# Twelve of sixteen weight conversions moved from the attention stage into the first layer after it, and the w_out conversions spread over 28 slots

## Chip, cores and metric

One core of one Trainium2 chip runs the whole program. The metric is the device time of one launch in microseconds, lower is better. Engines are named as the profile names them: PE (TensorE; PEld is its weight load), DVE (VectorE), ACT (ScalarE), POOL (GpSimd), SP (the engine that issues the DMAs here).

## The reference

Three stages follow each other. All arithmetic is float32, and the weights arrive as float64.

```python
scores = scale * np.matmul(q, k.transpose(0, 1, 3, 2))       # 4 batches, 8 heads, 576 x 576, head size 64
decay = cum[:, :, :, None] - cum[:, :, None, :]              # cum: running sum of log f
scores = np.where(causal, -1000000000.0, scores + decay)
attn = softmax(scores); out = np.matmul(attn, v)

h = x @ w_in                                                 # 2304 tokens, 512 -> 2048
g = h * np.tanh(softplus(h))
x = (g @ w_out)                                              # 2048 -> 512

a = x @ w1; b = x @ w2                                       # 512 -> 1024
h = a * b @ w3                                               # 1024 -> 1024
return (h @ w_out2)                                          # 1024 -> 512
```

## The kernel before, in words

The kernel has two phases. `phase_a` does the attention in 16 pairs of heads, four *slots* to a pair (`NU = 4`), and four slots more at the end. `phase_b` does the rest in two passes over half the tokens each; in the first of these passes `first_layer` multiplies x by w_in for the last two batches.

**A slot of phase A** (`slots`, L679 on of the file as it was) issues one third of a pair's scores and softmax (`score`: PE L339, DVE L360 to L367, ACT L370), the transposes of the block before (`turn`: PE L407, then copies out of PSUM on ACT and DVE, both L422), in every fourth slot the product with v and its scaling (`pv`: PE L441; `x_rows`: DVE L452, which needs the reciprocal sums `R`, sent to DRAM and back, L387 to L394), and *filler*: matmuls of later layers that PE does beside the softmax (`plan`: 24 to a slot, from slot 37 on 12, from slot 53 on 12 in every third slot). From slot 37 on the filler is `l1_unit` (L524), x times w_in for the second batch.

**A weight conversion** turns one piece of 128 x 512 numbers from float64 into float32. The float64 words are loaded as pairs of int32 (`cv_load`, L121, 512 KB). ACT scales the upper word (`cv_exp`, L132), three DVE instructions put sign, exponent and mantissa bits together (`cv_bits`, L140 to L142), and then either the result is stored to a scratch tensor (`cv_store`, L149, 256 KB) or it is used at once. In the trace the raw words of w_out are `cvru` and the result is `cvu`; for w1 and w2 they are `cvrv` and `cvv`.

**Slots are given to conversions by a table** in `phase_a`. `job(s, ...)` puts the load into slot s-1, ACT's part into slot s+lag, and the last step into slot s+lag+1. The loop that matters gives the 16 pieces of w_out and then the 16 pieces of w1 and w2 one after the other:

```python
for i in range(32):
    s = W_OUT_SLOT + int(W_OUT_STEP * i)      # 30 + int(1.08 i): slots 30 to 46, then 47 to 63
```

After each second w_out piece `sums_of` (POOL, L803 to L806) and two `build` calls form the seven operands of a Strassen-like product (ACT L822, POOL L823, store `ws<-pt` or `ws<-bs`, L824, 256 KB each) for a later layer. The operands pass through five staging places, so that ACT's L822 waits for the store that used its place before.

**The first layer of phase B** runs seven products for each of eight units m (`m_layer`, `m_order`: for each m the products 5, 6, 2, 3, 7, then product 1 of the next m, then product 4). A product is 12 matmuls. Products 1, 6, 7 and 4 of a unit accumulate in one PSUM bank; between them ACT copies it (L990, L994) or DVE adds it (L1000) to `Cx`. So product 4 cannot begin before DVE's add of product 7, and the only work of PE in between is product 1 of the next unit. Products 2 and 3 are added by DVE at L996 and L998. Beside this DVE forms the next unit's operand sums (`s_sums`, `sr` tiles, L1045 to L1050), ACT and POOL split them (`s_build`, L1057 and L1058), and the operands of the layer behind (`k_begin`, `g_l`, `y`) are begun. The pieces of w1 and w2 are read back from the scratch tensor only in the layer after the next (`gate_load`).

Order on an engine: PE's order is the order of the code; for the other engines and for SP's DMA queue the framework chooses the order when the kernel is built, within the priorities that the code gives. Each engine then runs its list in that order, and SP issues the DMAs one behind the other.

Of the kernel before, what the change touches and what calls it, by code (L numbers as in the profile page):

```python
# [9 lines left out]
F32 = mybir.dt.float32  # L10
F32R = mybir.dt.float32r
BF16 = mybir.dt.bfloat16
I32 = mybir.dt.int32
AF = mybir.ActivationFunctionType
# [9 lines left out]
NPAIR = NH // 2  # L24
# [8 lines left out]
NU = 4  # L33
# [15 lines left out]
L1_BOTH = 6  # L49
W_IN_STEP = 0.8  # L50
W_OUT_SLOT = 30
W_OUT_STEP = 1.08
L1_S = (21, 37)
SHARE = (26, 24, 22, 24)

# [9 lines left out]
def f32(ap):  # L65
    return ap.bitcast(F32)
# [4 lines left out]
F64_EXP = 2.0 ** -112  # L71
# [3 lines left out]
class Kernel:  # L75
# [79 lines left out]
    def rows(self, w, m):  # L155

        return w[128 * m:128 * m + 128]

    def l1_bank(self):
        self.nl1 += 1  # L160
        return self.ps_l[self.nl1 % len(self.ps_l)]
# [414 lines left out]
    def phase_a(self):  # L576
# [41 lines left out]
        def at(s, fn, *a):  # L618
            misc.setdefault(s, []).append((fn, a))
# [3 lines left out]
        def job(s, key, src, fin, *a, lag=1):  # L623
            at(max(0, s - 1), self.cv_load, key, src)
            conv.setdefault(s + lag, []).append(key)
            at(s + lag + 1, fin, *a)
# [4 lines left out]
        jobs = [(f"i{m}", self.cols(self.w_in, m), self.win_split, m) for m in range(DFF // 128)]  # L631
        for i, j in enumerate(jobs):
            job(W_IN_SLOT + int(W_IN_STEP * i), *j)
        for i in range(32):
            f = i % 16
            s = W_OUT_SLOT + int(W_OUT_STEP * i)
            if i < 16:
                u = i // 2
                job(s, f"u{u + 8 * (i % 2)}", self.rows(self.w_out, u + 8 * (i % 2)), int, lag=2)
                if i % 2:  # L640
                    at(s + 3, self.sums_of, 0, u)
                    for k in range(2):
                        at(s + 4 + k, self.build, 0, u, k)
            else:
                key, src = f"v{f}", self.cols((self.w1, self.w2)[f % 2], f // 2)
                job(s, key, src, self.cv_store, key, self.w12_scr[f], lag=2)
        at(32, self.x_places, 1)
        for p in range(4, 8):
            for half, s in ((0, (32, 33, 34, 36)), (1, (38, 38, 39, 40))):
# [1 line left out]
        for p in range(NPAIR):  # L651
            s = NU * p
# [407 lines left out]
    def first_layer(self, cover):  # L1060

        nc = self.nc
        T, self.vs = {}, {}
        self.sp = [[self.w_ring(f"sp{i}_{j}")[:, :1024] for j in range(2)] for i in range(2)]
        self.tmp = self.t_tile("tmp", F32).rearrange("p (k r w) -> p k r w", k=2, r=2)
        self.s_sums(0)
        self.x_operands(T, (1, 5))
        self.s_build(0, 0)
        self.x_operands(T, (6, 2))
        self.s_build(0, 1)  # L1070
        self.x_operands(T, (3, 7, 4))
        cover()

        def get(m, o):
            if o in (1, 2, 4):
                return self.wi[m + 8 if o == 4 else m], 0 if o == 1 else 256, 512
            return self.sp[m % 2][o in (7, 3)], 512 if o in (6, 3) else 0, 256

        def post(m, o, d, ps):
            if o == 3:  # L1080
                t = self.y[m] = self.big(0, f"y0_{m}")
                nc.scalar.activation(t.rearrange("p (r h w) -> p h r w", r=2, h=2), d[:, 0:2], AF.Mish)
            elif o == 4:
# [152 lines left out]
```

## Time and profile before

| | |
|---|---|
| median of 3 runs | 1009.26 us (1008.63 to 1011.7) |
| the profiled execution | 1007.64 us, of which its span 1005.8 us |
| PE busy | 896.9 us (89%) |
| DVE busy | 655.7 us (65%) |
| ACT busy | 502.3 us (50%) |
| POOL busy | 434.7 us (43%) |
| DMA | 185.99 MB, mean 185 GB/s |
| chain that ended last | PE 56%, DVE 13%, DMA 10%, ACT 5%, issue 4%, POOL 3% |

The busy shares are means over a program of unlike stages. PE is busy all through phase B and through the middle of phase A, and idles at the start, in the last third of phase A and where phase B begins. So the profile is read by stretches: which engine waits in this stretch, and what ended its wait. The attention stage ends at about 404 us, the first layer of phase B at about 523 us.

### The profile page before, as it was taken

The numbers are of one execution on the slowest core, as the hardware profiler recorded it, in microseconds if no ns is written. First come the engines' busy times: TensorE is split into PE (matmuls) and PEld (weight loads), VectorE is DVE, ScalarE is ACT, GpSimd is POOL, SyncE is SP. The second block draws the span as 40 slices with busy tenths as digits, with TensorE's granted clock in tenths as the row PEclk, the third lists the DMA queues.
The fourth block names the chain that finished last, engine by engine and source line by source line (L and its number), as shares of the span: only waits on it lengthen the run. The fifth ranks groups of instructions, "written<-read, shape, count | busy, mean of one in ns | idle before, by whom it ended". The sixth has DMA issues, their size and how long they took to land.

```text
span 1005.8 us, 17588 instructions
## 1 busy us (share of the span) xinstructions
PE 896.9 (89%) x6336; PEld 817.9 (81%) x6336; DVE 655.7 (65%) x1126; ACT 502.3 (50%) x1089; POOL 434.7 (43%) x414
## 2 busy tenths in 40 slices
PE   0699999999788678779999897899999989999998
PEld 0367767888566557769999897899999989999998
DVE  5997786647675656995327739666468954744472
ACT  2566675756665544435534445544464354422143
POOL 4657775325876100633304558455055453410042
PEclk9899999999989789989999999899999999999999
DMA  8457678748898974100045454754977435455551
GB/s 244 144 167 232 206 228 271 201 148 256 285 310 282 301 223 159 60 7 1 1 156 180 131 185 160 280 201 169 340 285 231 162 130 168 148 167 168 166 172 71
DMA packets 129350, 185.99 MB, mean 185 GB/s; under 512 B 12064, under 2 KB 75696, under 8 KB 129264
## 3 DMA queue, kind: packets, MB, share of 16 engines
q1 hardware_dynamic: 129264, 184.88, 56.6%
q8 instruction: 50, 0.82, 0.3%
q14 instruction: 36, 0.29, 0.1%
HBM read 129.33 MB, written 55.42 MB: 184 GB/s over the span
## 4 chain that ended last, share of the span: by engine, by line
PE 56%; DVE 13%; DMA 10%; ACT 5%; issue 4%; POOL 3%; SPq 1%; DVEq 0%; ACTq 0%; POOLq 0%
PE ps_x L985 15%; PE ps_x L913 11%; PE ps_z L985 7%; PE ps_y L913 5%; PE ps_z L913 5%; PE ps_l L524 5%; PE ps_y L985 4%; DMA cvrv<-in_w_dram 2%; DMA ws<-pt 2%; PE ps_s L339 2%; DVE g_l L886 1%; DMA cvri<-in_w_in_dram 1%; DMA cvru<-in_w_out_dram 1%; POOL pt L823 1%; PE ps_t L407 1%
## 5 line engine op out<-in xcount | busy, mean ns | idle before, releaser
L886 POOL TENSOR_TENSOR g_l<-y,g_h 128x576 fp32r<-128x576 f32 x48 | 74.9, 1563 | 88.8 <-ACT g_h L884 62.3
L524 PE MATMUL ps_l<-x,wi 128*128 128x288 f32 x672 | 104.4, 312 | 2.8 <-ACT h L531 2.8
L524 PEld LDWEIGHTS ps_l<-x,wi 128*128 128x128 f32 x672 | 96.4, 199 | 11.2 <-issue 6.0
L913 PE MATMUL ps_x<-g_h,ws 128*128 128x288 f32 x512 | 92.8, 299 | 2.4 <-ACT g_h L884 2.1
L886 POOL TENSOR_TENSOR h_l<-ab,h_h 128x576 fp32r<-128x576 f32 x24 | 35.7, 1487 | 126.6 <-ACT h_h L884 114.4
L884 ACT CAST g_h<-y 128x576 fp32r<-128x576 f32 x96 | 63.9, 674 | 52.9 <-PE ps_x L913 28.4
L886 DVE TENSOR_TENSOR g_l<-y,g_h 128x576 fp32r<-128x576 f32 x48 | 53.1, 1110 | 50.0 <-ACT g_h L884 46.3
L913 PEld LDWEIGHTS ps_x<-g_h,ws 128*128 128x128 f32 x512 | 76.8, 191 | 3.7 <-ACT g_h L884 2.8
L370 ACT ACTIVATE P<-P,sum 128x256 f32<-128x256 f32 (+3 forms) x112 | 70.4, 631 | 16.7 <-DVE sum L367 10.4
L339 PE MATMUL ps_s<-raw 64*128 64x128 f32 (+3 forms) x256 | 53.0, 493 | 17.2 <-DVE xr L452 10.1
L913 PE MATMUL ps_x<-g_l,ws 128*128 128x288 f32 x256 | 56.5, 302 | 11.1 <-DVE g_l L886 8.3
L339 PE MATMUL ps_s<-aug 64*128 64x128 f32 (+3 forms) x128 | 38.2, 576 | 24.7 <-DVE cvo L141 22.0
L985 PE MATMUL ps_x<-T,gs 128*128 128x288 f32 x384 | 55.6, 301 | 4.5 <-ACT Cg L990 3.7
L985 PEld LDWEIGHTS ps_x<-T,gs 128*128 128x128 f32 x384 | 53.3, 193 | 5.0 <-ACT Cg L990 3.9
L985 PE MATMUL ps_x<-T,ws 128*128 128x288 f32 x384 | 54.3, 296 | 2.3 <-ACT x L941 1.4
L360 DVE CUSTOM_DVE_ANT_0 P<-ps_s,m 128x256 f32<-128x256 f32 (+2 forms) x96 | 49.3, 552 | 8.6 <-PE ps_s L339 8.1
L985 PEld LDWEIGHTS ps_x<-T,ws 128*128 128x128 f32 x384 | 52.0, 188 | 3.0 <-ACT x L941 1.7
L407 PE MATMUL ps_t<-ident,P 128*128 128x128 f32 x288 | 41.4, 281 | 14.6 <-ACT pt L422 14.6
L913 PEld LDWEIGHTS ps_x<-g_l,ws 128*128 128x128 f32 x256 | 41.6, 191 | 13.0 <-DVE g_l L886 9.7
L422 DVE COPY pt<-ps_t 128x128 f32<-128x128 f32 (+1 forms) x64 | 29.6, 483 | 32.1 <-PE ps_t L407 31.8
L884 ACT CAST h_h<-ab 128x576 fp32r<-128x576 f32 x48 | 32.0, 674 | 36.9 <-PE ps_x L913 17.8
L490 PE MATMUL ps_l<-wo,w3h 128*128 128x512 f32 x128 | 45.4, 424 | 4.9 <-POOL wo L111 2.9
(269 smaller groups left out, 2445.0 us busy)
## 6 DMA issues: line engine op xcount, KB each, us to landing
ws<-ws SPq DMA_DIRECT2D x112, 512.0 KB
ws<-pt SPq DMA_DIRECT2D x67, 256.0 KB
ws<-gs SPq DMA_DIRECT2D x56, 256.0 KB
h_scr<-h SPq DMA_DIRECT2D x64, 144.0 KB
y<-h_scr SPq DMA_DIRECT2D x16, 576.0 KB
cvrt<-in_w3t_dram SPq DMA_DIRECT2D x16, 512.0 KB
cvri<-in_w_in_dram SPq DMA_DIRECT2D x16, 512.0 KB
cvru<-in_w_out_dram SPq DMA_DIRECT2D x16, 512.0 KB
```

Source lines behind the costliest of these rows:

```text
L339: mm(ps[:, 512 * hh:512 * hh + n], t[r, q0:q0 + 128], t[r, 0:n], start=first, stop=not first)
L360: dve = ttr(P[hh][:, :n], ps[:, 512 * hh:512 * hh + n], self.m1[:, 512 - n:], -0.125, 3.0e38, ALU.add, ALU.min, st[hh])
L370: ins = nc.scalar.activation(t[:, :n], t[:, :n], AF.Exp, bias=b, scale=-1.0, accum_out=self.sums[:, i:i + 1])
L407: tr(self.ps_t[hh][:, o + 128 * k:o + 128 * k + 128], P[:, 128 * k:128 * k + 128], self.ident)
L422: return copy(dst[:, 0:c + 1, 128 * c:128 * c + 128], src)
L490: mm(o, w, x, start=i == 0, stop=i == 23)
L524: mm(o[:, :TB], w, x, start=i == 0, stop=i == 11)
L823: nc.gpsimd.tensor_tensor(lo, x, f32(hi), ALU.subtract)
L884: self.nc.scalar.copy(hi, raw)
L886: eng.tensor_tensor(lo, raw, f32(hi), ALU.subtract)
L913: mm(ps[:, r, :TB], w[:, 256 * a + 128 * e:256 * a + 128 * e + 128], ops[i][b][:, r], start=o in (1, 5, 2) and f == 0 and (a, b) == (0, 0) ...
L985: mm(bank[:, r, :TB], w[:, i:i + 128], T[o, k][:, b, r], start=o in (1, 2, 5) and (k, a, b) == (0, 0, 0), stop=(k, a, b) == (1, 1, 0), ski ...
```

## The change

The 16 pieces of w_out are now spread over slots 30 to 57 (`W_OUT_STEP` 1.8). Of the pieces of w1 and w2 only the first four (`V_SOON`) are converted in phase A, in slots 56, 58, 60 and 62. The other twelve are converted in `first_layer`, two in each unit from the second to the seventh. The raw words of an even piece go into `tmp`, a tile that the layer's operand preparation no longer needs by then (one tile, so that the next load waits until the piece before is converted); those of an odd piece go into two half tiles (`vw`) of a ring of 12, and the odd conversions are done in halves. The results (`vt`) come from the same ring, which also holds the `sr` tiles. All DMAs stay on SP's queue.

```diff
-W_OUT_STEP = 1.08
+W_OUT_STEP = 1.8
+V_SOON = 4
...
+    def v_load(self, f):
+
+        src = self.v_src(f)
+        if f % 2 == 0:
+            self.vw[f] = [self.tmpw[:, :1024]]
+            self.nc.sync.dma_start(self.tmpw[:, :1024].rearrange("p (c w) -> p c w", c=4), src)
+            return
+        self.vw[f] = [self.x_tile(f"vw{f}_{i}", I32)[:, :512] for i in range(2)]
+        for i, raw in enumerate(self.vw[f]):
+            self.nc.sync.dma_start(raw.rearrange("p (c w) -> p c w", c=2), src[:, 2 * i:2 * i + 2])
+
+    def v_convert(self, f):
+
+        out = self.x_tile(f"vt{f}", F32)[:, :512]
+        raws = self.vw.pop(f)
+        n = 512 // len(raws)
+        for i, raw in enumerate(raws):
+            t = out[:, n * i:n * i + n]
+            self.cv[f, i] = raw, t
+            hw = raw.rearrange("p (n w) -> p n w", w=2)[:, :, 1]
+            self.nc.scalar.activation(t, f32(hw), AF.Copy, scale=F64_EXP)
+            self.cv_bits((f, i))
+        self.nc.sync.dma_start(self.w12_scr[f], out)
...
-        for i in range(32):
-            f = i % 16
+        for i in range(16):
             s = W_OUT_SLOT + int(W_OUT_STEP * i)
...
-                key, src = f"v{f}", self.cols((self.w1, self.w2)[f % 2], f // 2)
-                job(s, key, src, self.cv_store, key, self.w12_scr[f], lag=2)
+        for f in range(V_SOON):
+            job(NU * NPAIR - 8 + 2 * f, f"v{f}", self.v_src(f), self.cv_store, f"v{f}", self.w12_scr[f])
...
+            f = V_SOON + 2 * m
+            if o == 1 and m and f <= 16:
+                self.v_convert(f - 2)
+            if o == 1 and f < 16:
+                self.v_load(f)
+                self.v_load(f + 1)
+            if o == 3 and m and f <= 16:
+                self.v_convert(f - 1)
```

PE's list is the same in both kernels, instruction for instruction. The other lists change in phase A from slot 30 on and in the first layer. Line numbers of the changed kernel are 26 to 29 higher.

**Place 1, SP's queue late in phase A.** `R12` and `R13` are the reciprocal sums that DVE's L452 waits for, `cvrv` a load of raw words of w1 or w2, `w12_scr` the store of a converted piece, `aug`, `raw` and `va` the inputs of a coming pair. Before, around pair 12:

```order
L149 DMA w12_scr_65<-cvv3_3482 128x512
L121 DMA cvrv7_3574<-in_w2_dram 128x4x256
L316 DMA aug0_93<-cum_scr_67 2x576
L314 DMA aug0_93<-cum_scr_67 2x576
L317 DMA aug0_93<-cum_scr_67 2x64
L306 DMA raw1_92<-in_qk_dram 64x512
L318 DMA aug1_94<-cum_scr_67 2x512
L532 DMA h_scr_61<-h1_0_1_3570 128x288
L303 DMA raw1_92<-in_qk_dram 64x2x576
L392 DMA R12_3576<-inv_scr_66 64x576
L393 DMA R12_3576<-inv_scr_66 64x512
L394 DMA R12_3576<-inv_scr_66 64x64
```

With the change, around pair 13, where the loads of the four early pieces stand:

```order
L416 DMA inv_scr_66<-inv13_3581 9x128
L421 DMA R13_3627<-inv_scr_66 64x576
L422 DMA R13_3627<-inv_scr_66 64x512
L423 DMA R13_3627<-inv_scr_66 64x64
L850 DMA ws0_62<-pt_86 256x1x256 x3
L122 DMA cvrv2_3715<-in_w1_dram 128x4x256
L850 DMA ws0_62<-bs0_6_3_3621 128x512
L150 DMA w12_scr_65<-cvv0_3588 128x512
L122 DMA cvrv3_3796<-in_w2_dram 128x4x256
L353 DMA va15_3802<-in_v_dram 128x4x128
```

Before, piece 7 was loaded here ahead of pair 12's sums; now only piece 2 is loaded after pair 13's, and stores of w_out operands (`ws0`) stand in a place where there were none.

**Place 2, DVE at the start of the first layer**, the adds of products 2, 3 and 7 of unit 0 (`Cx_0` with `ps_y`, `ps_z`, `ps_x0`). Before:

```order
L996 TENSOR_TENSOR Cx_0_4303<-Cx_0_4303,ps_y_4089 128x576
L1050 TENSOR_TENSOR sr1_3_4320<-sr1_0_4317,sr1_2_4319 128x256
L1048 TENSOR_TENSOR sr2_2_4414<-sr2_2_4414,sr2_0_4412 128x256
L886 TENSOR_TENSOR TX4_1_4178<-tmp_4097,TX4_1_4178 128x576
L998 TENSOR_TENSOR Cx_0_4303<-Cx_0_4303,ps_z_4090 128x576
L1047 TENSOR_TENSOR sr3_2_4524<-sr3_1_4523 128x256
L1049 TENSOR_TENSOR sr3_3_4525<-sr3_0_4522,sr3_1_4523 128x256
L1045 TENSOR_TENSOR sr4_0_4632<-wi4_1424 128x512
L1045 TENSOR_TENSOR sr4_1_4633<-wi12_1877 128x512
L1000 TENSOR_TENSOR Cx_0_4303<-Cx_0_4303,ps_x0_4087 128x576
```

With the change:

```order
L1071 TENSOR_TENSOR sr2_1_4322<-wi10_1808 128x512
L1074 TENSOR_TENSOR sr1_2_4223<-sr1_2_4223,sr1_0_4221 128x256
L1022 TENSOR_TENSOR Cx_0_4207<-Cx_0_4207,ps_y_3993 128x576
L1073 TENSOR_TENSOR sr2_2_4323<-sr2_1_4322 128x256
L1075 TENSOR_TENSOR sr2_3_4324<-sr2_0_4321,sr2_1_4322 128x256
L912 TENSOR_TENSOR TX4_1_4082<-tmp_4001,TX4_1_4082 128x576
L1076 TENSOR_TENSOR sr1_3_4224<-sr1_0_4221,sr1_2_4223 128x256
L1074 TENSOR_TENSOR sr2_2_4323<-sr2_2_4323,sr2_0_4321 128x256
L1024 TENSOR_TENSOR Cx_0_4207<-Cx_0_4207,ps_z_3994 128x576
L1026 TENSOR_TENSOR Cx_0_4207<-Cx_0_4207,ps_x0_3991 128x576
```

The operand sums of units 3 and 4 that stood ahead of the add of product 7 now come later, since the ring of their tiles is shared with the conversions.

**Place 3, DVE in the middle of the first layer**, around the adds of unit 3. Before:

```order
L996 TENSOR_TENSOR Cx_2_4508<-Cx_2_4508,ps_y_4089 128x576
L998 TENSOR_TENSOR Cx_2_4508<-Cx_2_4508,ps_z_4090 128x576
L1000 TENSOR_TENSOR Cx_2_4508<-Cx_2_4508,ps_x0_4087 128x576
L879 TENSOR_TENSOR y0_2_4601<-y0_2_4601 128x2x288
L880 TENSOR_TENSOR y0_2_4601<-y0_10_4654,y0_2_4601 128x2x288
L996 TENSOR_TENSOR Cx_3_4618<-Cx_3_4618,ps_y_4089 128x576
L998 TENSOR_TENSOR Cx_3_4618<-Cx_3_4618,ps_z_4090 128x576
L1000 TENSOR_TENSOR Cx_3_4618<-Cx_3_4618,ps_x1_4088 128x576
```

With the change (`vt10`, `vt11` are pieces 10 and 11, `tmp` and `vw11` their raw words):

```order
L1022 TENSOR_TENSOR Cx_3_4569<-Cx_3_4569,ps_y_3993 128x576
L1071 TENSOR_TENSOR sr6_0_4845<-wi6_1502 128x512
L1071 TENSOR_TENSOR sr6_1_4846<-wi14_2017 128x512
L141 TENSOR_SCALAR vt10_4724<-vt10_4724 128x512
L141 TENSOR_SCALAR vt11_4808<-vt11_4808 128x256 x2
L1024 TENSOR_TENSOR Cx_3_4569<-Cx_3_4569,ps_z_3994 128x576
L1073 TENSOR_TENSOR sr6_2_4847<-sr6_1_4846 128x256
L1075 TENSOR_TENSOR sr6_3_4848<-sr6_0_4845,sr6_1_4846 128x256
L142 SCALAR_TENSOR_TENSOR vt10_4724<-tmp_4001,vt10_4724 128x512
L142 SCALAR_TENSOR_TENSOR vt11_4808<-vw11_0_4600,vt11_4808 128x256
L142 SCALAR_TENSOR_TENSOR vt11_4808<-vw11_1_4601,vt11_4808 128x256
L1026 TENSOR_TENSOR Cx_3_4569<-Cx_3_4569,ps_x1_3992 128x576
```

Before, the three adds stood one behind the other; now operand sums and parts of two conversions stand between them.

## Rows read from the trace of the kernel before

**Rows 1.** Busy time by stretch (columns: PE, PEld, DVE, ACT, POOL, clock, DMA share, GB/s)

```profile
200.00:244.00 44.00, 44.00 (x346) 38.76 (x344) 23.81 (x64) 24.82 (x76) 17.61 (x23) 1.00 0.62 190
244.00:334.00 90.00, 74.86 (x523) 59.23 (x520) 60.04 (x155) 60.11 (x182) 59.29 (x76) 0.93 0.90 291
334.00:404.00 70.00, 54.20 (x369) 41.52 (x367) 42.97 (x113) 31.54 (x92) 1.46 (x2) 0.88 0.69 218
...
442.00:523.00 81.00, 80.08 (x584) 79.85 (x585) 39.49 (x62) 38.67 (x58) 19.85 (x14) 0.97 0.07 26
```

**Rows 2.** What PE waited for, 244 to 404 us (total us, times, longest)

```profile
PE ps_t L407 <- ACT pt L422: 14.6, 7, 4.2
PE ps_s L339 <- DVE xr L452: 10.1, 4, 4.7
PE ps_s L339 <- DMA cvrv<-in_w_dram: 2.0, 1, 2.0
```

**Rows 3.** PE's timeline (start, us, in brackets the idle time before and its releaser)

```profile
251.94 2.81 PE L441 MATMUL ps_s<-pt,va 128*64 128x256 f32 x24
...
296.89 1.54 PE L407 MATMUL ps_t<-ident,P 128*128 128x128 f32 x6 [2.88 <-ACT pt L422]
...
367.98 1.16 PE L407 MATMUL ps_t<-ident,P 128*128 128x128 f32 x6 [4.24 <-ACT pt L422]
369.06 4.16 PE L441 MATMUL ps_s<-pt,va 128*64 128x256 f32 x24
...
385.62 2.81 PE L441 MATMUL ps_s<-pt,va 128*64 128x256 f32 x24
...
391.12 1.09 PE L407 MATMUL ps_t<-ident,P 128*128 128x128 f32 x8 [2.58 <-ACT pt L422]
...
400.72 2.81 PE L441 MATMUL ps_s<-pt,va 128*64 128x256 f32 x24
```

**Rows 4.** What ACT waited for, 244 to 404 us

```profile
ACT cvv L132 <- DMA cvrv<-in_w_dram: 25.4, 9, 7.0
ACT pt L822 <- DMA ws<-pt: 20.0, 18, 2.8
```

**Rows 5.** What DVE waited for, 244 to 404 us

```profile
DVE xr L452 <- DMA R<-inv_scr: 13.0, 4, 5.2
```

**Rows 6.** The conversions' instructions, by tile (ns: least, median, most; first and last start)

```profile
L132 ACT ACTIVATE cvv<-cvrv x16: 658/672/696, 320.4 to 394.7; 128x512 f32<-128x512 f32 x16
L140 DVE TENSOR_SCALAR cvv<-cvv x16: 416/421/478, 321.1 to 398.1; 128x512 int32<-128x512 int32 x16
L141 DVE SCALAR_TENSOR_TENSOR cvv<-cvrv,cvv x16: 678/686/697, 321.6 to 398.5; 128x512 int32<-128x512 int32 x16
L142 DVE SCALAR_TENSOR_TENSOR cvv<-cvrv,cvv x16: 631/688/1098, 322.7 to 399.2; 128x512 int32<-128x512 int32 x16
...
L141 DVE SCALAR_TENSOR_TENSOR cvu<-cvru,cvu x16: 674/694/1198, 217.1 to 310.5; 128x512 int32<-128x512 int32 x16
```

**Rows 7.** DMA issues by tile, with the size of each

```profile
cvrv<-in_w_dram SPq DMA_DIRECT2D x16, 512.0 KB
...
w_scr<-cvv SPq DMA_DIRECT2D x16, 256.0 KB
```

**Rows 8.** Busy time in the first layer's beginning (columns as in rows 1)

```profile
442.00:449.00 7.00, 6.93 (x36) 6.93 (x37) 7.00 (x16) 2.49 (x4) 1.36 (x1) 0.65 0.00 0
```

**Rows 9.** Timelines of PE, DVE and POOL in the first layer

```profile
442.07 3.25 PE L985 MATMUL ps_x<-TX,wi 128*128 128x288 f32 x12 [5.87 <-DVE Cx L1000]
...
452.30 1.76 PE L985 MATMUL ps_x<-TX,sp 128*128 128x288 f32 x12
...
442.61 0.41 DVE L1047 TENSOR_TENSOR sr<-sr 128x256 f32<-128x256 f32 x1
...
446.91 1.28 DVE L1045 TENSOR_TENSOR sr<-wi 128x512 f32<-128x512 f32 x2
...
472.06 1.29 POOL L1058 TENSOR_TENSOR sp<-sr,sp 128x512 fp32r<-128x512 f32 x1 [2.99 <-ACT sp L1057]
```

More of the change, by code (lines that the diff above doesn't have):

```diff
@@ L157, in rows, with v_src @@
         return w[128 * m:128 * m + 128]
+    def v_src(self, f):
+        return self.cols((self.w1, self.w2)[f % 2], f // 2)
+    def v_load(self, f):
[18 more added lines that the diff above has]
+        self.nc.sync.dma_start(self.w12_scr[f], out)
     def l1_bank(self):
@@ L633, in phase_a @@
             job(W_IN_SLOT + int(W_IN_STEP * i), *j)
-        for i in range(32):
-            f = i % 16
+        for i in range(16):
             s = W_OUT_SLOT + int(W_OUT_STEP * i)
[L637 to L644, printed above, removed]
-                key, src = f"v{f}", self.cols((self.w1, self.w2)[f % 2], f // 2)
-                job(s, key, src, self.cv_store, key, self.w12_scr[f], lag=2)
+            u = i // 2
+            job(s, f"u{u + 8 * (i % 2)}", self.rows(self.w_out, u + 8 * (i % 2)), int, lag=2)
+            if i % 2:
+                at(s + 3, self.sums_of, 0, u)
+                for k in range(2):
+                    at(s + 4 + k, self.build, 0, u, k)
+        for f in range(V_SOON):
+            job(NU * NPAIR - 8 + 2 * f, f"v{f}", self.v_src(f), self.cv_store, f"v{f}", self.w12_scr[f])
         at(32, self.x_places, 1)
@@ L1064, in first_layer @@
         self.sp = [[self.w_ring(f"sp{i}_{j}")[:, :1024] for j in range(2)] for i in range(2)]
-        self.tmp = self.t_tile("tmp", F32).rearrange("p (k r w) -> p k r w", k=2, r=2)
+        self.tmpw, self.vw = self.t_tile("tmp", I32), {}
+        self.tmp = f32(self.tmpw).rearrange("p (k r w) -> p k r w", k=2, r=2)
         self.s_sums(0)
```

## The prediction

> **What bounds the kernel now.** I read the busy time by stretches first, then the waits of PE in the stretch that changes, then what its releasers had themselves waited for. In the last two fifths of the attention stage, from slot 37 at 244 us to its end at 404 us, PE is busy for 74.86 of 90 and 54.20 of 70 us and idle for 30.9 [rows 1]. No engine is full there: DVE has 103 of 160 us, ACT 92, POOL 61. The DMA is nearest to full, 0.90 at 291 GB/s and then 0.69 at 218 GB/s. PE's waits end on ACT's copies (14.6 us), on DVE's scaling of x (10.1) and once on SP behind a `cvrv` load (2.0) [rows 2]. Those engines wait on DMA: ACT stood 25.4 us before conversions of w1 and w2 whose words had not landed, and 20.0 us for stores that still held a staging place [rows 4]; DVE stood 13.0 us for the reciprocal sums [rows 5]. So PE waits for transfers, at second hand. It pays twice, since the granted clock falls with the waits: 0.93 and 0.88 as means of the two stretches [rows 1], and the same 24 matmuls take 4.16 us after the wait of 4.24 at 367.98, and 2.81 us elsewhere [rows 3]. Adding such differences up over the stretch gives 11 us, below the 15 that the two means allow (0.07 x 90 + 0.12 x 70).
>
> The first layer, from 442 us, is another case: PE is busy 80.08 of 81 us, DVE and ACT about half, the DMA at 0.07 [rows 1]. There the question is only whether anything comes between two products.
>
> **The change, part by part.**
>
> *Out of the attention stage.* Twelve conversions leave. Each is 0.67 us of ACT, 0.42 + 0.69 + 0.69 = 1.8 us of DVE [rows 6], and 768 KB of transfers and two issues on SP [rows 7]. In all 8 us of ACT, 21.6 of DVE and 9.4 MB. The stretch moves 41.5 MB now (291 x 90 + 218 x 70). The slower w_out table puts three of its 512 KB loads later than slot 37, 1.6 MB, and moves no operand build across that slot. That leaves 33.7 MB, 116 us at 291 GB/s, against 160 now. PE's own work is 160 - 30.9 - 11 = 118 us. So 42 us is the most that can go, and nothing the least if the same instructions find other reasons to wait. What goes I take by cause:
>
> - Waits behind conversions of w1 and w2. Those of 4.24 and 2.58 us [rows 3], the 2.0 [rows 2] and two under 1 us come to 10.2. Twelve of sixteen loads go, and the other four come every second slot instead of nearly every slot: 8 of 10.2.
> - Waits on DVE's scaling, 10.1 us [rows 2]. The longest, 4.7, came where `R12` stood in SP's queue behind a store of piece 3 and a load of piece 7; with the change the loads of `R13` follow its store directly (place 1). I take 6.5.
> - Waits on ACT's copies while ACT stood before a staging place, like the 2.88 at 296.89 [rows 3]: what these two items leave of the 30.9 but for 1.4 of others, 9. The builds now take 27 slots instead of 16, so five of nine go: 5.
> - Clock given back with these: 7 of 11.
> - New waits: builds now stand in slots 50 to 62, where there were none, and with less filler PE sooner meets the softmax chain. Nothing prices this directly; the nearest row is the pair from 369.06 to 385.62, 16.6 us with PE hardly waiting [rows 3], which is what a pair without filler costs here, against 12 to 14 of PE's own. The bounds are 0 and the 9 of the third item; I take 3.5, since the builds come at 0.6 of the old rate.
>
> Sum: -8 - 6.5 - 5 - 7 + 3.5 = **-23 us**. As a cross-check, the seven pairs from the product with v at 251.94 to the last at 400.72 [rows 3] take 148.8 us now; at 19.5, 19, 19, 18, 18, 16 and 15 us they would take 124.5.
>
> *Into the first layer.* The twelve conversions cost the same 1.8 us of DVE and 0.67 of ACT, in six units of 7 products at 1.6 us, the 1.76 of a row less its overlap with the next [rows 9], 11.2 us. Of such a unit DVE now needs half and ACT half [rows 1], so 3.6 and 1.3 us more fit, and so do 2 x 768 KB through an idle DMA. Hidden by PE's products, then, as long as the order leaves room, and it is tight: DVE's add of product 7 has only product 1 of the next unit as its cover, 1.6 us. In place 3 the parts between the adds of products 2 and 3 cost 1.28 + 0.42 + 0.5 = 2.2 us and those between 3 and 7 another 2 x 0.4 + 0.69 + 2 x 0.35 = 2.2 [rows 6, 9], half-size pieces at about half. Both adds come late, and product 4 of unit 3 waits some 1.9 us. The same count gives 0.5 for unit 2, 0.9 for unit 4, about 1.2 for unit 5, nothing for 1 and 6. Bounds 0 (DVE is idle half of the time and may run ahead) and 6 x 4.6 (rival 2). I take the count: **+4.5**.
>
> *At its start* something goes that the change does not mean. PE waited 5.87 us for the add of product 7 of unit 0 [rows 9], behind four operand sums, and then ran at a clock of 0.65 for 7 us [rows 8], 0.35 x 7 = 2.4 us lost. With place 2 the add follows that of product 3. By the durations it would end at about 437.9 instead of 442.0: -4.1, and -2.4 with the clock: **-6.5** (bounds 0 and -8.3).
>
> *Elsewhere.* The last stores ahead of phase B come earlier, worth 0.3 at most. The late pieces are read back only two layers later, so that nobody waits for the later end of the conversions.
>
> Sum: -23 + 4.5 - 6.5 = **-25 us**. From the profiled execution, 1007.6, that is 982.6. The median of the runs is 1.6 above the profiled one, so I expect **984 us**.
>
> *A rule that speaks against this.* The longest L141 of `cvu`, with POOL at work, took 1.20 us, the longest of `cvv`, with POOL idle, 0.70 [rows 6]. In the first layer POOL runs two subtractions of 1.29 us in each unit [rows 9]. The Trainium skill (SBUF — State Buffer, "Who interferes with whom") says that a DVE instruction with two SBUF inputs contends with a GpSimd instruction that reads SBUF, and that the second to issue blocks until the first is done. By that rule eight of a unit's conversion instructions can each be held for what is left of a subtraction; the trace agrees, and an estimate by it and the row's half microsecond is 0.6 us more in each of six units, +8 instead of +4.5, and 988 us. Rival 2 takes the same to its end from rows alone.
>
> **The rivals.**
>
> 1. *Half.* PE in the attention stage is held by the chain from scores through softmax to transposes, and by staging places, not by the loads that go. For it: ACT's 20.0 us before staging places [rows 4] remain in kind, over more slots. Against: from 200 to 244 us PE is busy all the time, with a DMA share of 0.62 [rows 1]. Then the first item and 3 of the clock go, and the first layer's two terms cancel: -11, 998 us.
> 2. *Slower: the conversions hold the first layer.* Place: DVE's add of product 7, in six units. Two conversions (3.6 us) and two stretches of 1.3 in which DVE is held beside POOL's subtractions [rows 6, 9] make 6.2 us ahead of it, 1.6 covered: 4.6 of wait, and 2.4 of low clock as after the wait at the start, 7 for each unit, 42 in all. With -23 and -6.5 this ends 12.5 above, at 1022 us. It decides from 29.5 / 6 = 4.9 us for a unit on. Against it: the list interleaves, so that rarely more than 2.2 us of foreign work stand before an add.
> 3. *All of it.* The DMA was the only cause, PE's 42 us go, the start gains and the middle costs nothing: -48, 961 us.
> 4. *No change.* The w_out builds in slots 50 to 62 put as much before ACT and SP as the loads did: PE waits as before, within 3 us of 1009.
>
> **How the numbers follow.** Forecast 0.62, half 0.19, all 0.07, no change 0.06, slower 0.06. A difference under 0.3%, 3 us, cannot be told from none. Faster by more than that: 0.62 + 0.19 + 0.07 = 0.88; the same 0.06; slower 0.06. The range reaches from 970 (the first four items in full, -38.8 in all) to 1001, beyond rival 1; outside lie rivals 2 to 4, 0.19 together.
>
> **What would show it.** Between slot 37 and the end of attention, PE's idle time falls from 30.9 to about 14 us and the stretch from 160 to about 137, with a clock above 0.96 and no wait of ACT on `cvrv` over 2 us. The wait of 5.87 falls under 2 and the first layer's start keeps its clock. In units 2 to 5 PE waits 1 to 2 us on DVE's add of product 7, and nowhere else. Wrong would be: PE's waits in attention moved to staging places or sums (rivals 1 and 4); over 4 us of wait in each unit (rival 2).

## The result, and the profile after

The changed kernel takes 994.72 us (median of 4 runs, 990.74 to 996.85) against 1008.94 us of the kernel before (1007.91 to 1011.7): a ratio of 0.985, 95% interval 0.981 to 0.9891, so 14.2 us faster where 25 were forecast. The profiled execution took 993.02 us, its span is 990.9 us.

Three points of PE's list cut the program into the terms of the forecast: product 1 of unit 0 (the first L1011 of the layer; L985 before), product 4 of unit 0, the one that waited 5.87 us [rows 9], and product 4 of unit 7.

| us | before | after | difference | forecast |
|---|---|---|---|---|
| product 1 of unit 0 starts | 420.79 | 395.76 | -25.0 | -23 |
| from there to product 4 of unit 0 | 21.28 | 16.39 | -4.9 | -4.1 |
| from there to product 4 of unit 7 | 79.80 | 94.86 | +15.1 | +4.5 - 2.4 |
| from there to the end of the span | 483.9 | 483.9 | 0 | 0 |

Two terms came about as forecast. The third took back 15.1 us, or 17.5 with the 2.4 of clock counted apart as in the forecast, where it was priced at 4.5. First the attention: busy time by stretch in the profile after (columns as in rows 1), answering to [rows 1].

```profile
244.00:328.00 84.00, 80.29 (x590) 63.84 (x588) 58.86 (x156) 55.74 (x178) 46.14 (x58) 0.96 0.77 244
328.00:377.60 49.60, 41.09 (x306) 31.07 (x302) 28.81 (x78) 26.14 (x82) 19.28 (x24) 0.97 0.73 241
377.60:412.00 34.40, 28.94 (x180) 28.07 (x180) 32.93 (x56) 14.48 (x31) 19.22 (x15) 0.85 0.19 62
412.00:508.00 96.00, 82.89 (x583) 81.48 (x584) 69.61 (x122) 47.99 (x79) 26.14 (x16) 0.93 0.36 112
```

The attention from slot 37 takes 133.6 us instead of 160, PE is idle for 12.2 of them (133.6 less 121.38 busy) instead of 30.9, and the clock is at 0.96 and 0.97. The last row is the first layer. There PE was busy for all but a microsecond [rows 1], and now stands for 13 of 96; the clock fell to 0.93, and DVE's busy time there rose from 39 us [rows 1] to 70. What PE, ACT and DVE waited for in the attention of the kernel after (total us, times, longest), answering to [rows 2, 4, 5]:

```profile
PE ps_t L440 <- ACT pt L451: 7.8, 2, 4.9
PE ps_t L436 <- ACT pt L451: 1.4, 2, 0.7
PE ps_s L368 <- DVE xr L481: 0.3, 1, 0.3
...
ACT pt L848 <- DMA ws<-pt: 15.6, 9, 6.8
ACT cvv L133 <- DMA w_scr<-cvv: 1.9, 1, 1.9
DVE xr L481 <- DMA R<-inv_scr: 7.4, 1, 7.4
```

Line numbers up to L150 are one higher than before, not 26 to 29: ACT's L132 is L133 here, and the bit instructions L140 to L142 are L141 to L143. ACT's 25.4 us before words of w1 and w2 are gone altogether, and so are the 10.1 us of PE on DVE's scaling, but for 0.3. The waits for a staging place (`ws<-pt`) stay, half as many but with a longer one among them, and with those for the other staged operand (`ws<-bs`, 6.43 us) they stand ahead of ACT's copies in PE's two longest waits there, 2.85 and 4.95 us of the 12.2. The 7.4 us of DVE come at the very end, before the last pair's scaling, and cost PE 2.82 us there. PE's timeline at the join and in the first layer of the kernel after:

```profile
379.79 3.22 PE L553 MATMUL ps_z<-x,wi 128*128 128x288 f32 x12 [2.82 <-DVE xr L481]
...
412.15 1.85 PE L1011 MATMUL ps_x<-TX,wi 128*128 128x288 f32 x12 [0.27 <-DVE Cx L1026]
...
436.63 1.85 PE L1011 MATMUL ps_x<-TX,wi 128*128 128x288 f32 x12 [1.68 <-DVE Cx L1026]
...
451.05 3.25 PE L1011 MATMUL ps_x<-TX,wi 128*128 128x288 f32 x12 [3.02 <-DVE Cx L1026]
...
464.21 1.86 PE L1011 MATMUL ps_x<-TX,wi 128*128 128x288 f32 x12 [0.35 <-DVE Cx L1026]
...
482.69 3.25 PE L1011 MATMUL ps_x<-TX,wi 128*128 128x288 f32 x12 [7.07 <-DVE Cx L1026]
```

The second of these rows is the one that waited 5.87 us. The last four are product 4 of units 2, 3, 4 and 5, each behind DVE's add of product 7: the place that was forecast, with 1.68, 3.02, 0.35 and 7.07 us where 0.5, 1.9, 0.9 and 1.2 were counted. After the two long ones the clock is at the lower of its two levels (the granted mean is 0.52 and 0.50 over those two rows, and 0.88 from 449 to 508 us), and the same twelve matmuls take 3.25 us instead of 1.85.

Two things stand ahead of those adds. The same stretch of the kernel after, timelines of SP's queue, ACT, DVE and POOL around the add of unit 2 and around that of unit 5:

```profile
429.95 0.38 SPq L169 DMA_DIRECT2D tmp<-in_w_dram  x1
434.27 0.66 ACT L184 ACTIVATE vt<-tmp 128x512 f32<-128x512 f32 x1 [4.49 <-DMA tmp<-in_w_dram]
434.97 0.94 DVE L141 TENSOR_SCALAR vt<-vt 128x512 int32<-128x512 int32 x3 [1.14 <-ACT vt L184]
435.83 0.75 DVE L1026 TENSOR_TENSOR Cx<-Cx,ps_x 128x576 f32<-128x576 f32 x1
...
469.31 1.48 POOL L912 TENSOR_TENSOR g_l<-y,g_h 128x576 fp32r<-128x576 f32 x1 [4.68 <-DVE vt L142]
470.75 1.47 POOL L1084 TENSOR_TENSOR sp<-sr,sp 128x512 fp32r<-128x512 f32 x1
472.18 1.89 POOL L912 TENSOR_TENSOR g_l<-y,g_h 128x576 fp32r<-128x576 f32 x1
469.40 1.67 DVE L142 SCALAR_TENSOR_TENSOR vt<-vw,vt 128x256 int32<-128x256 int32 x1
470.99 1.78 DVE L143 SCALAR_TENSOR_TENSOR vt<-tmp,vt 128x512 int32<-128x512 int32 x1
472.69 1.65 DVE L142 SCALAR_TENSOR_TENSOR vt<-vw,vt 128x256 int32<-128x256 int32 x1
474.27 0.41 DVE L143 SCALAR_TENSOR_TENSOR vt<-vw,vt 128x256 int32<-128x256 int32 x1
...
481.89 0.74 DVE L1026 TENSOR_TENSOR Cx<-Cx,ps_x 128x576 f32<-128x576 f32 x1
```

In unit 2 the load into `tmp` is issued only when the piece before it has been read, ACT can start on its words 4.3 us later, and DVE's first bit instruction and then the add stand in line behind ACT. In unit 5 three bit instructions of DVE take 1.67, 1.78 and 1.65 us, side by side with three subtractions of POOL; the fourth, with POOL done, takes 0.41.

### The profile page after: what moved, and what is told of

It reads as the page before. It is cut to its first block, busy times and chain, and to the rows that moved or that the text cites. A ratio compares the mean times of both kernels' runs of the same rounds, so it can differ in the third digit from the quotient of the medians.

```text
span 990.9 us, 17690 instructions
## 1 busy us (share of the span) xinstructions
PE 895.6 (90%) x6336; PEld 818.1 (83%) x6336; DVE 665.3 (67%) x1144; ACT 499.8 (50%) x1095; POOL 440.1 (44%) x414
## 4 chain that ended last, share of the span: by engine, by line
PE 61%; DVE 17%; DMA 9%; issue 5%; ACT 3%; SPq 2%; POOL 1%; DVEq 0%; ACTq 0%; POOLq 0%
PE ps_x L1011 13%; PE ps_x L939 11%; PE ps_z L1011 6%; PE ps_z L939 6%; PE ps_y L939 6%; PE ps_l L553 5%; PE ps_y L1011 3%; PE ps_s L368 3%; PE ps_l L519 3%; PE ps_s L470 2%; PE ps_t L436 2%; DMA ws<-pt 2%; DVE g_l L912 2%; DMA raw<-in_qk_dram 2%; DMA cvri<-in_w_in_dram 1%
## 5 line engine op out<-in xcount | busy, mean ns | idle before, releaser
L553 PE MATMUL ps_l<-x,wi 128*128 128x288 f32 x672 | 100.6, 304 | 3.3 <-ACT h L560 3.3
L553 PEld LDWEIGHTS ps_l<-x,wi 128*128 128x128 f32 x672 | 92.8, 193 | 12.3 <-issue 7.2
L1011 PE MATMUL ps_x<-T,gs 128*128 128x288 f32 x384 | 55.8, 301 | 4.3 <-ACT Cg L1016 3.5
L1011 PEld LDWEIGHTS ps_x<-T,gs 128*128 128x128 f32 x384 | 53.4, 193 | 4.9 <-ACT Cg L1016 3.7
L1011 PE MATMUL ps_x<-T,ws 128*128 128x288 f32 x384 | 54.3, 296 | 2.7 <-ACT x L967 1.8
L1011 PEld LDWEIGHTS ps_x<-T,ws 128*128 128x128 f32 x384 | 52.0, 189 | 3.3 <-ACT x L967 2.0
L939 PE MATMUL ps_x<-h_h,ws 128*128 128x288 f32 x256 | 46.4, 297 | 0.1
```

Source lines behind the costliest of these rows:

```text
L553: mm(o[:, :TB], w, x, start=i == 0, stop=i == 11)
L939: mm(ps[:, r, :TB], w[:, 256 * a + 128 * e:256 * a + 128 * e + 128], ops[i][b][:, r], start=o in (1, 5, 2) and f == 0 and (a, b) == (0, 0) ...
L1011: mm(bank[:, r, :TB], w[:, i:i + 128], T[o, k][:, b, r], start=o in (1, 2, 5) and (k, a, b) == (0, 0, 0), stop=(k, a, b) == (1, 1, 0), ski ...
```

## The experiments

Theory: the twelve conversions cost this much because of *what they stand beside*, a load that comes late in one tile (units 2 and 3) and POOL's subtractions, which hold DVE's instructions with two operands (unit 5). Rival: DVE simply has too much to do ahead of the adds, and the same work costs the same wherever it stands. For the attention, theory A says that taking pieces of w1 and w2 out gave the gain, rival B that thinning those of w_out did. A kernel with the attention's part as in the change starts its layer anywhere from 393.6 to 399.8 us in single profiles, so I compare the layer by its own length, from product 1 of unit 0 to product 4 of unit 7:

| kernel | median us | ratio, 95% interval | layer starts | length | PE idle | DVE busy |
|---|---|---|---|---|---|---|
| before | 1008.94 | | 420.79 | 101.08 | 9.97 | 60.70 |
| after | 994.72 | 0.985 (0.981 to 0.9891) | 395.76 | 111.25 | 16.10 | 85.84 |
| spread only | 1000.58 | 0.9927 (0.9887 to 0.9967) | 415.51 | 99.53 | 7.88 | 58.13 |
| move only | 996.58 | 0.9859 (0.9819 to 0.99) | 394.98 | 111.94 | 16.78 | 85.21 |
| twelve left out | 985.03 | 0.9752 (0.9712 to 0.9793) | 399.77 | 102.06 | 10.58 | 59.89 |
| tmp behind product 7 | 990.14 | 0.9795 (0.9752 to 0.9838) | 395.00 | 106.56 | 14.21 | 83.31 |
| g_l on DVE | 990.56 | 0.9821 (0.9792 to 0.985) | 393.56 | 107.57 | 15.85 | 84.08 |
| eight early | 991.79 | 0.9827 (0.9788 to 0.9866) | 396.44 | 105.72 | 12.29 | 76.57 |
| both of these: eight early, tmp | 992.25 | 0.983 (0.9801 to 0.986) | 400.78 | 108.09 | 10.96 | 74.94 |
| the same, w_out dense | 998.51 | 0.9897 (0.9874 to 0.9919) | 403.77 | 108.55 | 13.61 | 75.30 |
| tmp and g_l | 988.84 | 0.9778 (0.9742 to 0.9815) | 396.38 | 104.20 | 12.76 | 82.31 |
| g_l and sp on DVE | 987.20 | 0.9771 (0.9736 to 0.9805) | 393.92 | 104.33 | 11.42 | 85.52 |
| all three | 982.87 | 0.9722 (0.9695 to 0.975) | 394.68 | 100.73 | 9.76 | 84.23 |
| before, g_l and sp on DVE | 1008.58 | 0.9995 (0.9978 to 1.0013) | 420.56 | 101.45 | 7.62 | 66.82 |

(Length, PE and DVE from the busy time of exactly that stretch in each profile; idle is the length less PE's busy time. Each ratio is to runs of the kernel before on the same chip.)

**The two halves of the change.** *Spread only:*

```diff
-V_SOON = 4
+V_SOON = 16
-            job(NU * NPAIR - 8 + 2 * f, f"v{f}", ...)
+            job(W_OUT_SLOT + int(1.08 * (16 + f)), f"v{f}", ..., lag=2)
```

> The sixteen pieces of w1 and w2 stay in the attention, in the sub-slots that they had before; only the pieces of w_out are spread by 1.8. If the gain of the attention comes from taking the twelve pieces of w1 and w2 out of it (theory A, mine: two stores and two loads fewer in flight between sub-slots 48 and 64), spreading alone gives 0 to -4 us, 1005 to 1009 us, and the wait of PE on the transposes behind the v loads stays near its 8 us. If it comes from thinning the pieces of w_out (rival B), the attention ends some 10 to 20 us earlier and the time is 990 to 1000 us. Since both rows of pieces now lie in the same sub-slots, up to 10 us slower (1015 to 1020) would speak for A as well. The first layer has no conversion in it and its wait at the start stays near 5.9 us.

*Move only* (`W_OUT_STEP` back to 1.08):

> The pieces of w_out keep their old step of 1.08; only the twelve pieces of w1 and w2 are in the first layer. Theory A (the move carries the gain): the attention ends within 5 us of the changed kernel's, 995 to 1000 us in all. Rival B (the spread carries it): the waits of the first half of the w_out pieces stay, the attention gains only 8 to 12 us of the 26, and the time is 1009 to 1014 us, no better than before, since the first layer still costs its 15 us. The first layer should be the same as in the changed kernel under both, within 1.5 us from its first product to the first product of k.

Busy time from 328 to 380 us, first with the spread only, then with the move only:

```profile
328.00:380.00 52.00, 39.65 (x248) 28.44 (x249) 42.37 (x102) 32.32 (x94) 22.66 (x27) 0.84 0.97 302
```

```profile
328.00:380.00 52.00, 50.98 (x390) 40.73 (x390) 31.34 (x93) 28.22 (x91) 1.53 (x3) 0.98 0.40 129
```

With the sixteen pieces of w1 and w2 left in place the DMA is full in this stretch (0.97) and PE stands 12 of 52 us; with twelve of them gone PE is busy throughout. The move alone brings the layer's start 25.8 us forward, as much as the whole change, and theory A holds for it. The seven pairs up to the last product with v take 126.5 us then, against 148.8 before; in the seven profiles whose attention is that of the change they take 122.4 to 127.3, so that what the spread adds to the move cannot be told from nothing.

But the spread alone, which I gave 0 to 4 us, brings 9.3 by the medians. PE with the spread only, and two of ACT's waits up to the end of its attention:

```profile
388.19 2.81 PE L470 MATMUL ps_s<-pt,va 128*64 128x256 f32 x24
...
396.64 3.22 PE L553 MATMUL ps_z<-x,wi 128*128 128x288 f32 x12 [5.52 <-DVE xr L481]
```

```profile
ACT cvv L133 <- DMA w_scr<-cvv: 15.4, 5, 4.5
...
ACT cvv L133 <- DMA cvrv<-in_w_dram: 2.4, 2, 1.7
```

The last product with v starts 12.5 us earlier than at 400.72 [rows 3], inside rival B's 10 to 20; 7.2 of it are lost again before the layer's first product, most of them in the wait of 5.52. ACT's 25.4 us before words of w1 and w2 are 2.4 though all sixteen loads stayed, but 15.4 us before the stores of converted pieces have come instead. PE's waits on DVE's scaling, 10.1 us before, are 5.4 with the spread only, 5.6 with the move only and 0.3 with both. So neither theory holds alone: the move is enough, and the spread without it gives a part.

The first layer is the same in the changed kernel and in the move only, so the two show how far one profile can be trusted. Product 4 of units 2 to 5 with the move only:

```profile
436.12 3.06 PE L1011 MATMUL ps_x<-TX,wi 128*128 128x288 f32 x12 [1.91 <-DVE Cx L1026]
...
450.42 1.85 PE L1011 MATMUL ps_x<-TX,wi 128*128 128x288 f32 x12 [1.36 <-DVE Cx L1026]
...
464.17 1.85 PE L1011 MATMUL ps_x<-TX,wi 128*128 128x288 f32 x12 [2.16 <-DVE Cx L1026]
...
483.08 3.25 PE L1011 MATMUL ps_x<-TX,wi 128*128 128x288 f32 x12 [7.53 <-DVE Cx L1026]
```

The lengths agree within 0.7 us (111.25 and 111.94) and so do the waits of unit 5, while those of units 3 and 4 differ by 1.7 and 1.8 us, and their sum over units 2 to 4 by 0.4.

**The price of the twelve conversions.** *Twelve left out:* the loads and conversions in the layer are taken out, and the gate reads an early piece in place of each late one.

> Left out: the conversion of the twelve late pieces of w1 and w2; the gate reads one of the four early pieces in place of each, so the output is another. It prices all that the twelve conversions cost in the first layer, and bounds what any better place for them could give. If the 15 us that the first layer grew are the conversions' (theory), 994.7 - 15 to 17 = 978 to 980 us, with no wait of PE over 0.6 us on the add of product 7 in units 2 to 5. If a part of it comes from the layer starting earlier (rival: weights and states that the layer loads land later against its start), only 5 to 10 us go, 985 to 990 us, and the waits in units 3 or 5 stay without a conversion ahead of them.

```profile
421.14 3.25 PE L1011 MATMUL ps_x<-TX,wi 128*128 128x288 f32 x12 [5.88 <-DVE Cx L1026]
...
435.36 1.86 PE L1011 MATMUL ps_x<-TX,wi 128*128 128x288 f32 x12 [0.46 <-DVE Cx L1026]
```

That is PE in the layer without conversions: units 2 to 5 wait for nothing, and from product 4 of unit 0 to that of unit 7 it takes 80.7 us instead of 94.9, so the conversions cost 14.2 there, as theory had it. But the time was 985, not 979, for a reason that neither had: the wait of unit 0 is back, 5.88 us. It is the conversions that had removed it. Their tiles share a ring with the operand sums `sr`, and so those sums no longer stood ahead of unit 0's add; in this kernel they do again. (Its layer also starts 4.0 us later than in the changed kernel, and what comes behind the layer is 3.7 us shorter; these two nearly cancel.) The net price of the twelve in this layer is 9.2 us (111.25 - 102.06).

**The late load.** *tmp behind product 7:*

```diff
             if o == 1 and m and f <= 16:
-                self.v_convert(f - 2)
+                self.v_convert(f - 1)
             if o == 1 and f < 16:
-                self.v_load(f)
+                if m == 0:
+                    self.v_load(f)
                 self.v_load(f + 1)
-            if o == 3 and m and f <= 16:
-                self.v_convert(f - 1)
+            if o == 7 and f < 16:
+                self.v_convert(f)
+                if f + 2 < 16:
+                    self.v_load(f + 2)
```

> The piece that uses the tile tmp is converted in the step behind product 7 rather than behind product 1, and its next load is issued there, half a unit before it is read; the odd piece is converted behind product 1. Theory 1 (units 2 and 3 wait because the load into the one tmp tile is issued only when the piece before was read, and ACT, DVE and the add of product 7 queue behind it: 1.7 + 3.0 us of PE's wait): those two go, the wait of unit 5 stays, 989 to 991 us. Theory 2 (the wait is the conversion's own work on DVE, wherever it stands): the wait moves to the adds of product 3 or of the next unit, and the time stays at 993 to 996 us. Slower, 997 to 1000 us: the conversion behind product 7 now stands ahead of the splits for the next unit.

ACT and PE of that kernel, the same pieces in units 2, 3 and 5:

```profile
430.36 0.67 ACT L184 ACTIVATE vt<-tmp 128x512 f32<-128x512 f32 x1 [1.84 <-DMA tmp<-in_w_dram]
435.22 1.85 PE L1011 MATMUL ps_x<-TX,wi 128*128 128x288 f32 x12 [1.01 <-DVE Cx L1026]
...
448.22 1.85 PE L1011 MATMUL ps_x<-TX,wi 128*128 128x288 f32 x12 [1.62 <-DVE Cx L1026]
...
478.39 3.21 PE L1011 MATMUL ps_x<-TX,wi 128*128 128x288 f32 x12 [7.52 <-DVE Cx L1026]
```

990.14 us, inside theory 1. ACT still waits for the load, but less, and at another point of the unit. The waits of units 2 and 3 fell from 4.70 to 2.63 us, not to nothing; unit 3 keeps its full clock (1.85 instead of 3.25), and the layer is 4.7 us shorter. Unit 5 is where it was. Units 2 and 3 alone would not show it, since they waited 3.27 us with the move only and the load as late as before; units 2 to 4 together waited 5.05 and 5.43 us with the late load and 2.63 here, and the layer's length says the same. The medians do not decide it: the interval of the ratio overlaps that of the changed kernel.

**POOL beside DVE.** *g_l on DVE:* the three subtractions of the next layer's first operands that POOL did in unit 5 (the rows at 469.31 and 472.18 are two of them).

```diff
-        self.halves(raw, hi, lo, k)
+        self.halves(raw, hi, lo, 1 if name.startswith("g0_1_") and k < T_AHEAD + 2 else k)
```

> Three subtractions g_l that GpSimd does beside the conversions of units 5 and 6 (operands of the next layer, 1.5 to 1.9 us each there) go to DVE, where such a one takes 0.75 us. Theory C (unit 5's wait of 7.1 us comes from DVE's two-input instructions being held beside GpSimd: 1.67 + 1.78 + 1.65 + 1.95 where 0.42 + 0.68 + 0.42 + 0.75 is their time alone, 4.8 us too much): the stretched instructions go back to their time where no subtraction sp stands beside them, DVE gets 2.2 us more work and loses about 3 to 4 us of stretching, the wait falls to 4 to 6 us, 992 to 994 us. Rival D (too much work in DVE's queue ahead of the add of product 7: six us of conversion and the operands of the next layer): the wait stays or grows by up to 2 us, 994 to 997 us.

DVE, POOL and PE of that kernel, the same piece in unit 5:

```profile
468.40 0.42 DVE L142 SCALAR_TENSOR_TENSOR vt<-vw,vt 128x256 int32<-128x256 int32 x1
...
469.40 0.69 DVE L143 SCALAR_TENSOR_TENSOR vt<-tmp,vt 128x512 int32<-128x512 int32 x1
470.01 0.42 DVE L142 SCALAR_TENSOR_TENSOR vt<-vw,vt 128x256 int32<-128x256 int32 x1
...
469.43 3.15 POOL L1084 TENSOR_TENSOR sp<-sr,sp 128x512 fp32r<-128x512 f32 x1 [8.56 <-ACT sp L1083]
477.78 2.90 PE L1011 MATMUL ps_x<-TX,wi 128*128 128x288 f32 x12 [3.57 <-DVE Cx L1026]
```

DVE was given 2.2 us more to do and was done sooner. The three instructions that took 5.1 us take 1.53, and the wait of unit 5 is halved, a little more than theory C had it (4 to 6 us). Rival D falls as the only cause: more work cannot be done sooner in a queue that is merely too long. The 990.56 us lie below what I gave theory C (992 to 994), and for another reason than the wait: units 3 and 4 now wait 3.42 and 2.14 us (3.02 and 0.35 in the changed kernel, 1.36 and 2.16 with the move only), so that PE's idle time in the layer hardly fell (16.10 to 15.85), while its busy time fell by 3.4: the twelve matmuls after unit 3's wait kept the full clock (1.86 us instead of 3.25), and those after unit 5's had part of it (2.90).

**Fewer late pieces.** *Eight early* (`V_SOON` 8, early slots 48 + 2f) and two kernels on top of it:

> Eight pieces of w1 and w2 are converted in the attention, one in every second sub-slot from 48, and eight in the first layer, in units 1 to 4; otherwise as in the changed kernel. Rival D (DVE's queue in unit 5 holds conversions and the next layer's operands at once): unit 5 has no conversion, its wait of 7.1 us falls under 1 us, the waits of units 2 and 3 (1.7 and 3.0 us) stay, and the attention pays 1 to 4 us for four more pieces: 988 to 991 us. If the wait of unit 5 were the next layer's operands alone, it stays over 5 us and the time is 995 to 999 us.

> Eight pieces in the attention as in the run with eight early ones, and the piece in tmp converted behind product 7, loaded half a unit earlier. Theory: both effects add up, the late load (4.6 us measured) and unit 5's queue (6 to 7 us), less 1 to 4 us in the attention: 983 to 987 us. Rival: the two share what they win, 988 to 990 us.

> The run before with the step of the w_out pieces back at 1.08, so that they end at sub-slot 47 and the eight early pieces of w1 and w2 begin at 48: no two pieces are in one sub-slot. Theory (what the attention pays is two pieces at once): the attention ends as early as in the changed kernel, 982 to 986 us, 1 to 3 us under the run before. Rival (the pieces of w_out want to be far apart): 2 to 4 us more than the run before, 986 to 990 us.

With eight early the wait of unit 5 is gone, as there is no conversion in it, but those of units 3 and 4 are 4.39 and 2.31 us, and 2.9 us are won by the medians (991.79; 988 to 991 were expected), which the intervals do not tell from nothing. Neither of the other two did what I expected. With tmp behind product 7 as well, 992.25: units 3 and 4 wait 3.16 and 3.48 us, the layer's clock is 0.91, and the attention ended later. With the w_out pieces dense, 998.51: the supposition that only pieces in one sub-slot harm each other was wrong, since DVE's waits on the reciprocal sums grew from 6.7 to 16.1 us in the attention, and PE stood behind them:

```profile
DVE xr L481 <- DMA R<-inv_scr: 16.1, 5, 5.7
PE ps_s L368 <- DVE xr L481: 9.3, 4, 4.1
```

Why unit 3 waits longer when fewer pieces follow is not settled by these runs; the 2.31 us of unit 4 are hardly more than the 2.16 with the move only.

**Together, and against the kernel before.**

> The piece in tmp converted behind product 7 (as in the run that did this alone) and three subtractions g_l on DVE (as in the run that did that alone). Alone they gave 4.7 us in units 1 to 5 and 3.5 us in the wait of unit 5. Theory (two causes, each with its own place): they add up, 8 us off the layer, the wait of unit 5 at 3 to 4.5 us, no other over 1.7 us, 985 to 988 us. Rival (both only shift DVE's queue, which is too long by the same amount): 989 to 992 us, no better than either alone.

Nearly the sum: the layer is 7.05 us shorter where 4.69 and 3.68 apart would make 8.4; the median, 988.84 us, lies just above what was expected. It was taken on a chip where the kernel before took 1011.72 us; by its ratio it is 986.5 beside the 1008.94 here, as theory had it. Unit 5 still waits 4.68 us, beside the subtractions `sp` that POOL kept. Those were next:

```diff
-        self.nc.gpsimd.tensor_tensor(v[:, :, 1], x, f32(v[:, :, 0]), ALU.subtract)
+        (self.nc.vector if m > 2 else self.nc.gpsimd).tensor_tensor(v[:, :, 1], x, f32(v[:, :, 0]), ALU.subtract)
```

> As the run with three subtractions g_l on DVE, and in units 2 to 6 the subtractions sp of the next unit's weight sums on DVE as well, so that GpSimd does nothing beside the conversions. Theory C in full (GpSimd's subtractions hold DVE's two-input instructions): no bit instruction of the conversions over 0.75 us, no addition of 576 over 0.8 us in units 3 to 5, DVE's work grows by 1.4 us a unit and loses about 2 us of stretching, 988 to 990.5 us. Rival D (DVE's queue is what is long): every unit from 3 on waits 0.5 to 1.5 us more, 992 to 996 us.

> All three: the piece in tmp behind product 7, three subtractions g_l and ten subtractions sp on DVE. Theory C: 983 to 987 us, the lowest of all kernels here that compute the reference. Rival D: 988 to 992 us, above the run without the sp subtractions.

987.20 and 982.87 us, both just below theory C's ranges and far from rival D's: the second is the fastest kernel here, with an interval that lies wholly below that of the changed kernel. Its PE in the layer, and its bit instructions on DVE, grouped by shape (count, busy us, mean ns, idle before):

```profile
422.31 1.86 PE L1011 MATMUL ps_x<-TX,wi 128*128 128x288 f32 x12 [1.73 <-DVE Cx L1026]
434.32 1.84 PE L1011 MATMUL ps_x<-TX,wi 128*128 128x288 f32 x12 [0.59 <-DVE Cx L1026]
447.18 1.86 PE L1011 MATMUL ps_x<-TX,wi 128*128 128x288 f32 x12 [1.46 <-DVE Cx L1026]
472.04 3.19 PE L1011 MATMUL ps_x<-TX,wi 128*128 128x288 f32 x12 [2.28 <-DVE Cx L1026]
```

```profile
L142 DVE SCALAR_TENSOR_TENSOR vt<-vw,vt 128x256 int32<-128x256 int32 x12 | 4.7, 414 | 0.0
L143 DVE SCALAR_TENSOR_TENSOR vt<-tmp,vt 128x512 int32<-128x512 int32 x6 | 4.1, 680 | 0.0
```

The changed kernel's groups, in the same view:

```profile
L142 DVE SCALAR_TENSOR_TENSOR vt<-vw,vt 128x256 int32<-128x256 int32 x12 | 8.4, 713 | 0.0
L143 DVE SCALAR_TENSOR_TENSOR vt<-tmp,vt 128x512 int32<-128x512 int32 x6 | 5.2, 863 | 0.0
```

The layer with its twelve conversions is now as short as it was without them before (100.73 against 101.08, which has the wait of 5.87 us in it). DVE does 9.05 us more (ten subtractions at 0.68 and three at 0.75), and its busy time is not longer but 1.6 us shorter. So some 9 to 11 us of it had been spent held: 10.7 by the busy times, which leave out where two instructions overlap, and 9.4 if the groups of equal shape are compared one by one.

> The kernel before, without the change, but with the thirteen subtractions on DVE as in the fastest kernel. Theory (GpSimd's subtractions cost only because the conversions fill DVE: DVE is busy 60.7 of the 101.1 us that the layer took before): nothing to gain here, 1006 to 1010 us, the layer within 1.5 us of its 101.1. Rival (the thirteen subtractions are better on DVE whatever else runs, and the fastest kernel owes its gain over the changed one to that): 1000 to 1004 us, the layer 4 to 8 us shorter.

1008.58 us, a ratio of 0.9995 (0.9978 to 1.0013): in the kernel before, the same thirteen subtractions on DVE change nothing. (PE idles 2.35 us less in its layer and is busy 2.72 us longer, at a clock of 0.93 instead of 0.97.) So POOL's subtractions cost nothing where DVE is busy for 60% of the layer and no conversion stands ahead of the adds, and the fastest kernel owes its gain to the pairing with the conversions, which fill DVE to 77% (85.84 of 111.25). From which share on they cost, no run here shows.

## Why the prediction was right in its direction and short in its size

- **Attention, -23.** Measured -25.0 at the layer's first product. The seven pairs take 122.4 us where the cross-check had 124.5. The main cause was right: with the conversions of w1 and w2 went ACT's waits on their words. How the rest divides is not shown. The waits on the reciprocal sums were put down to those conversions' place in SP's queue, but with the move only DVE still stood 7.7 us before the sums and PE 5.6 us behind it; and the 5 us put down to the spread of the builds are not borne out, since the move alone gives the whole gain within what profiles differ.
- **Start of the layer, -6.5.** The wait of 5.87 us went to 0.27, and this stretch is 4.9 us shorter where 4.1 were worked out; the clock's 2.4 came back too, since the row that took 3.25 takes 1.85. Leaving the conversions out brought the wait back, so that the order was indeed the reason.
- **Into the first layer, +4.5: this is the step that failed.** From unit 0 to unit 7 PE stands 12.1 us longer (12.96 idle against 0.85) and is busy 2.95 us longer, +15.1 in all where 4.5 less the 2.4 of clock were forecast. With that 2.4 counted apart the term is +17.5: 12.1 of waits and 5.4 of low clock behind them. Place and engine were right, and also that no unit but 2 to 5 would wait. Three things were mis-sized. The conversions were priced at their undisturbed time, 1.8 us of DVE, though the text named POOL's subtractions as what could hold them: unit 5 was counted at 1.2 us and waited 7.07. The load into `tmp` was taken as hidden by an idle DMA, but with one tile it is issued only after the last read of the piece before, and ACT starts on it 4.3 us later: units 2 and 3 waited 4.7 instead of 2.4. And a wait in the layer was priced without the clock that follows it: the 5.4 us.
- **The rule that spoke against it** was priced beside the sum and not in it. The Trainium skill (SBUF — State Buffer, "Who interferes with whom") says that a DVE instruction with two SBUF inputs contends with a GpSimd instruction that reads SBUF. The trace agrees with the rule, in the rows of 1.67, 1.78 and 1.65 us and in the run that took the subtractions away. By the estimate from it the term was +8 and the time 988; measured are +17.5, the 2.4 of clock counted apart, and 994.72. The estimate had 0.6 us for a unit; in unit 5 those three rows alone are 3.6 us longer than without the subtractions (5.10 against 1.53).
- **The rivals.** Rival 2 named the mechanism of what went wrong and put it in all six units at 7 us each; only unit 5 came to that and past it (7.07 of wait where the rival had 4.6, and the low clock behind it). Rival 1 gave nearly the right time (998) for a wrong reason: the attention did not give half, it gave all, and the layer took it back. The range of 970 to 1001 held the result because rival 1 lay within it; as what rival 1 describes did not happen, that was luck.

## What to carry to other kernels

Work that is moved into a stretch where an engine is half idle can cost more than its own time if another engine works beside it, as POOL's subtractions did beside DVE's conversions: look at what runs *beside* the new instructions, and price them at their held duration. Moving the short subtractions from GpSimd to the fuller engine made the layer 3.7 to 6.9 us shorter there, and nothing shorter in the kernel before, without the conversions. A tile that is loaded again for each piece should have its next load issued where the following read is half a stage away, not behind the last one, and the price of a wait ahead of PE can include slow matmuls after it.

## What the runs showed of the hardware that was not expected

- Two engines that share the work can be slower than one: three instructions of DVE took 5.1 us beside three subtractions of POOL (4.84 us), 9.9 us of engine time, for what takes DVE alone 1.53 (with g_l on DVE) and 2 x 0.75 + 0.68 = 2.18 us (in the fastest kernel). POOL is held as well: the same `sp` subtraction took 1.29 us [rows 9] and up to 3.15 in the run with g_l on DVE.
- The clock after a wait: twelve matmuls took 3.25 us after waits of 3.02 and 7.07 us in the changed kernel, but 1.86 after 3.42 and 2.90 after 3.57 with g_l on DVE, and 3.19 after only 2.28 in the fastest kernel. The length of one wait thus does not settle whether it costs the clock; what does stays open.
